# Float32 attention for tiles 3 to 5, and TensorE transposes for the normalized rows of tiles 0 to 2, in a fused attention and gated MLP kernel

## The chip, the cores and the metric

One core of one Trainium2 chip runs the kernel. The metric is the device time of one execution in microseconds. Times inside an execution are counted from the start of its span. Engines are named as in the profile: PE is TensorE, DVE is VectorE, ACT is ScalarE, POOL is GpSimd, SP is SyncE, which issues most transfers.

## The reference

Attention over 4 batches of 8 heads, 768 rows of 64 elements: each row sees its neighbours within 15 rows and 24 block summaries (the elementwise maximum of k over 32 rows, with the mean of v). The result, 3072 tokens of 512 elements, is normalized and goes through a gated MLP.

```python
k_sum = k.reshape(B, H, nb, block, D).max(axis=3)            # block 32, nb 24
v_sum = v.reshape(B, H, nb, block, D).mean(axis=3)
scores_l = np.where(abs(i - j) < 16, scale * q @ k.T, -1e9)  # per batch and head
scores_s = scale * q @ k_sum.T + np.log(block)
a = softmax(concatenate([scores_l, scores_s], axis=-1))
x = (a @ concatenate([v, v_sum], axis=2)).reshape(B * S, H * D)   # heads side by side
xn = x / sqrt(mean(x * x) + 1e-6) * rms_g
g = xn @ w_gate                                              # 512 -> 1536
out = (g * sigmoid(g) * (xn @ w_val)) @ w_out                # 1536 -> 512
```

## The kernel before

The tokens are cut into 24 tiles of 128 rows, six for each batch. A tile passes through scores, softmax and the weighted sum, in two halves of four heads each, then through the normalization (norm_a, norm_b), which leaves its transposed rows in the buffer xT as f16 high and low halves. The MLP takes the tokens in groups of 384, 128, 256 and six times 384; a group has twelve gate_val steps (24 matmuls, 12 for the gate and 12 for the value) and twelve project steps. So the first gate_val needs norm_b of tiles 0, 1 and 2, the first group.

A tile is computed in one of two ways.

- Tiles 0 to 2 (SU = 3) in float32, by the su_ steps. su_k and su_q transpose k and q on PE against an identity. su_scores (matmul L921, masked maximum on DVE at L925, subtraction of the maximum on POOL), su_expo (exponentials on ACT at L934 and L935, then six transposes on PE at L940 and L942, copied out of PSUM by ACT and DVE) and su_attend (matmuls L957 and L960, then three DVE instructions) follow, once for each half. The operands v2f (the rows beside the tile and the v means) are filled by POOL's own transfers (L664), four for each tile, and by su_vsum.
- Tiles 3 to 23 in f16 high and low halves. q, k and v are scaled and split (prep_q, prep_k, prep_v), and k, q and the exponentials are transposed by DMA (kT from khl, qT from qs, eT from ee); the matmuls are L753 in scores and L794 in attend.

The scale of the f16 halves of a batch comes from sums of squares. For batch 0 they are the twelve su_square instructions on ACT (L838), added up on PE at L622; L642 transposes the k maxima back to rows. norm_b of every tile makes high and low halves of the rows (xs, by ACT and by POOL) and transposes them by a DMA on the SP queue (L994).

The gate and value weights sit in the buffer w_gv, in twelve slots of 1024 columns. decode_gv (ACT L457, DVE L458 and L459) and split_gv (PE L493 and L496, ACT L487 and L506, DVE L507) fill one slot each, as the weights come in.

All steps stand in the list PLAN, and tables in ORDER then fix the order of the instructions on each engine; each engine works strictly in that order. ENG says which engine runs a step. The buffers of the first stage are in the pool "start", which is given up before the first gate_val. Among the later buffers the f16 tiles have one for the masked scores (sm) and one for the exponentials (ee), and three PSUM banks named att are shared by all attention steps.

Of the kernel before, what the change touches and what calls it, by code (L numbers as in the profile page):

```python
# [8 lines left out]
F32 = mybir.dt.float32  # L9
# [10 lines left out]
P = 128  # L20
# [9 lines left out]
SU = 3  # L30
SMB = 1
# [3 lines left out]
    sfill="v", susm="p", v2q="p", wgv="a", wo="a", wolo="v", wlo="v", xlo="p", xs="a", w_pow2="p",  # L35
# [16 lines left out]
sum_fold 1 0 0 0; sum_fold 1 0 0 1; prep_k 4; decode_o 2; split_ks 0; decode_gv 5; split_gv 5; prep_q 3; prep_k 5;
fill_k 3; sum_load 1 0 0 2; sum_load 1 0 0 3; sum_load 1 0 1 0; load_gv 7; decode_o 4; decode_gv 6; sum_load 1 0 1 1;
load_o 6; scores 3 0; project 0 0 384 0; sum_fold 1 0 0 2; prep_v 3; gate_val 0 2 384; load_o 8; sum_fold 1 0 0 3;
gate_val 0 3 384; expo 3 0; decode_gv 7; load_gv 8; sum_load 1 0 1 2; load_unit 4; split_gv 6; fill_k 5; decode_o 6;
project 0 1 384 0; scores 3 1; expo 3 1; sum_fold 1 0 1 0; load_gv 9; sum_load 1 0 1 3; sum_fold 1 0 1 1;
sum_fold 1 0 1 2; sum_fold 1 0 1 3; load_o 10; project 0 2 384 0; split_gv 7; sum_load 1 1 0 0; gate_val 0 4 384;
sum_fold 1 1 0 0; sum_load 1 1 0 1; decode_gv 8; project 0 3 384 0; sum_load 1 1 0 2; fill_k 4; sum_scale 1 0;
prep_q 4; split_gv 8; sum_fold 1 1 0 1; sum_load 1 1 0 3; sum_fold 1 1 0 2; project 0 4 384 0; sum_load 1 1 1 0;
load_ks 1; gate_val 0 5 384; gate_val 0 6 384; sum_load 1 1 1 1; attend 3; norm_a 3; sum_fold 1 1 0 3;  # L60
sum_fold 1 1 1 0; project 0 5 384 0; load_unit 5; sum_fold 1 1 1 1; decode_gv 9; scores 4 0; decode_o 8; split_gv 9;
prep_q 5; sum_load 1 1 1 2; load_k 6; expo 4 0; sum_fold 1 1 1 2; split_ks 1; load_gv 10; load_gv 11;
gate_val 0 8 384; decode_gv 10; norm_b 3; gate_val 0 7 384; sum_load 1 1 1 3; scores 4 1; sum_fold 1 1 1 3;
decode_o 10; load_unit 6; swap_att 2; decode_gv 11; gate_val 1 0 128; prep_k 6; project 1 0 128 384; gate_val 1 1 128;
prep_v 4; load_k 7; gate_val 0 9 384; project 0 6 384 0; split_gv 10; project 1 1 128 384; prep_q 6; gate_val 1 2 128;
gate_val 1 3 128; split_gv 11; project 0 7 384 0; scores 5 0; expo 4 1; prep_k 7; fill_k 6; attend 4;
project 1 2 128 384; project 1 3 128 384; norm_a 4; swap_right; scale_h; scores 5 1; load_k 8; sum_load 2 0 0 1;
scores 6 0; scores 6 1; gate_val 1 4 128; load_unit 7; project 0 8 384 0; expo 5 0; sum_scale 1 1; expo 5 1;
project 1 4 128 384; gate_val 1 5 128; project 1 5 128 384; norm_b 4; gate_val 1 6 128; expo 6 0; project 1 6 128 384;
gate_val 1 7 128; expo 6 1; prep_q 7; gate_val 0 11 384; load_k 11; prep_v 5; attend 5; sum_load 2 0 0 0; prep_v 6;  # L70
gate_val 1 8 128; gate_val 0 10 384; project 1 7 128 384; prep_k 8; fill_k 7; norm_a 5; load_unit 8;
project 0 9 384 0; project 0 10 384 0; row_o 0; row_o 1; row_o 2; row_o 3; row_o 4; row_o 5; gate_val 1 9 128;
scores 7 0; gate_val 1 10 128; project 1 8 128 384; norm_b 5; gate_val 1 11 128; load_k 9; prep_q 8; attend 6;
project 1 9 128 384; project 1 10 128 384; scale_o; gate_val 2 0 256; expo 7 0; gate_val 2 1 256; prep_k 9;
swap_att 3; norm_a 6; gate_val 2 2 256; project 1 11 128 384; project 2 0 256 512; project 2 1 256 512; conv_o 0;
scores 7 1; sum_load 2 0 0 2; fill_k 8; project 2 2 256 512; sum_fold 2 0 0 0; sum_fold 2 0 0 1; load_unit 9;
scores 8 0; sum_load 2 0 0 3; load_k 10; prep_v 7; expo 7 1; sum_load 2 0 1 0; sum_load 2 0 1 1; gate_val 2 3 256;
norm_b 6; scores 8 1; gate_val 2 5 256; prep_q 9; project 2 3 256 512; conv_o 1; sum_fold 2 0 0 2; expo 8 0;
sum_fold 2 0 0 3; prep_k 10; prep_k 11; gate_val 2 4 256; expo 8 1; attend 7; sum_load 2 0 1 2; norm_a 7;
gate_val 2 6 256; norm_b 7; prep_v 8; fill_k 10; project 0 11 384 0; sum_fold 2 0 1 0; project 2 4 256 512;  # L80
project 2 5 256 512; conv_o 2; attend 8; fill_k 9; gate_val 2 7 256; sum_fold 2 0 1 1; norm_a 8; project 2 6 256 512;
gate_val 2 8 256; sum_fold 2 0 1 2; norm_b 8; scores 9 0; sum_load 2 0 1 3; gate_val 2 9 256; gate_val 2 10 256;
expo 9 0; sum_load 2 1 0 0; load_unit 10; project 2 7 256 512; conv_o 3; prep_q 10; gate_val 2 11 256; scores 9 1;
sum_fold 2 0 1 3; sum_scale 2 0; gate_val 3 0 384; project 2 8 256 512; sum_load 2 1 0 1; sum_fold 2 1 0 0; load_ks 2;
project 2 9 256 512; conv_o 4; expo 9 1; gate_val 3 1 384; project 2 10 256 512; load_unit 11; split_ks 2;
project 2 11 256 512; conv_o 5; project 3 0 384 768; sum_fold 2 1 0 1; sum_load 2 1 0 2; sum_fold 2 1 0 2;
# [190 lines left out]
def body(tc, q, k, v, wg, wv, wo, rg, out):  # L277
# [19 lines left out]
    with ExitStack() as ctx:  # L297
# [336 lines left out]
        def load_ks(b):  # L634
# [6 lines left out]
            for g in range(NC):  # L641
                nc.tensor.transpose(pt[0:NB, g * P:(g + 1) * P], ks32[:, g, :], ident)  # L642
# [445 lines left out]
```

## Time and profile before

| | |
|---|---|
| time, median of 3 runs | 752.61 us (750.48 to 753.82) |
| profiled execution, own time | 751.9 us |
| its span | 750.1 us |
| mean granted clock of PE | 0.964 |
| PE busy | 685.6 us (91%) |
| DVE busy | 517.5 us (69%) |
| ACT busy | 440.2 us (59%) |
| POOL busy | 260.9 us (35%) |

The own time of the profiled execution holds the span and 1.8 us around it. Busy shares are means over the whole span: what bounds the kernel is seen by stages. The first gate_val starts at 76.12 us; the gate results of the following steps reach DVE (L1014) from 81.14 us on, the ninth at 158.76, the 31st at 254.65, the 43rd at 317.91.

### The profile page before, as it was taken

To read this page: it belongs to the slowest core of one execution; us is meant where nothing else is said; L and a number is where in the kernel's file an instruction comes from. 1 tells how busy PE (TensorE), PEld (TensorE's weight loads), DVE (VectorE), ACT (ScalarE), POOL (GpSimd) and SP (SyncE) were. 2 spreads that over 40 slices of the span, in tenths; PEclk is the share of its full clock that TensorE was granted. 3 is DMA by queue.
4 is the path that set the end of the run, shared out by engine and by line. 5 is a ranking of instruction groups with operands and counts; after the bars stand their busy time and mean duration, and the time that the engine had idled before them with its cause. 6 is when DMAs were issued, how large, how long until landed. Compare 5 with 4: busy or idle time off the path is not lost.

```text
span 750.1 us, 14300 instructions
## 1 busy us (share of the span) xinstructions
PE 685.6 (91%) x4978; PEld 437.7 (58%) x4978; DVE 517.5 (69%) x1507; ACT 440.2 (59%) x936; POOL 260.9 (35%) x347
## 2 busy tenths in 40 slices
PE   3973989388988999999999999999999999999997
PEld 2562556256767786556565556655656555655554
DVE  4598887797678989877678677577757655544223
ACT  2589858776587867756566574657555543522111
POOL 8174113565244564553332253523223312210000
PEclk9995899699999999999999999999999999999999
DMA  9956996559956956687686676765566632221001
GB/s 217 291 197 211 234 254 190 120 108 195 179 94 128 190 119 163 138 174 141 119 168 144 147 155 144 128 138 116 125 113 105 108 78 40 39 50 43 1 0 43
DMA packets 270548, 100.23 MB, mean 134 GB/s; under 512 B 254212, under 2 KB 254308, under 8 KB 270476
## 3 DMA queue, kind: packets, MB, share of 16 engines
q1 hardware_dynamic: 265212, 91.09, 58.0%
q10 hardware_dynamic: 3456, 6.29, 2.3%
q0 software_dynamic: 1808, 1.93, 1.3%
q8 instruction: 39, 0.64, 0.3%
q14 instruction: 33, 0.27, 0.1%
HBM read 51.38 MB, written 6.64 MB: 77 GB/s over the span
## 4 chain that ended last, share of the span: by engine, by line
PE 60%; DMA 9%; DVE 7%; ACT 7%; issue 3%; POOL 2%; SPq 1%; ACTq 0%; POOLq 0%; DVEq 0%
PE gv L1009 37%; PE acc L1038 18%; PE att L753 3%; DMA kT<-khl 2%; DMA eT<-ee 2%; PE att L794 2%; ACT sm L768 1%; DMA qT<-qs 1%; DVE sm L757 1%; DVE hl L357 1%; DMA sum<-hn 1%; POOL ee L357 1%; DMA hn<-in_v_dram 1%; DMA hn<-in_k_dram 1%; ACT ee L352 1%
## 5 line engine op out<-in xcount | busy, mean ns | idle before, releaser
L1009 PE MATMUL gv<-xT,w_gv 128*128 128x384 f16 (+2 forms) x2592 | 407.7, 312 | 13.2 <-DVE th L1014 7.5
L1009 PEld LDWEIGHTS <-w_gv 128*128 128x128 f16 x2592 | 242.5, 99 | 158.9 <-issue 24.1
L1038 PE MATMUL acc<-wo,hh 128*128 128x512 f16 (+1 forms) x576 | 177.0, 389 | 0.0
L357 POOL TENSOR_TENSOR ee<-sm,ee 128x512 f16<-128x512 f32 (+1 forms) x84 | 83.1, 1006 | 134.8 <-ACT ee L352 120.1
L1038 PE MATMUL acc<-wo,hl 128*128 128x512 f16 (+1 forms) x288 | 111.1, 386 | 3.4 <-DVE hl L357 3.4
L1013 ACT ACTIVATE th<-gv,gains 128x384 f32<-128x384 f32 (+2 forms) x108 | 58.2, 539 | 82.2 <-PE gv L1009 78.3
L352 ACT CAST hh<-th 128x384 f16<-128x384 f32 (+3 forms) x108 | 50.8, 470 | 88.0 <-DVE th L1016 44.6
L768 ACT ACTIVATE sm<-sm,mx,c 128x192 f32<-128x192 f32 x168 | 81.6, 537 | 31.2 <-DVE mx L760 22.1
L1014 DVE SCALAR_TENSOR_TENSOR th<-th,gv 128x384 f32<-128x384 f32 (+2 forms) x108 | 54.5, 505 | 64.4 <-ACT th L1013 64.0
L357 DVE TENSOR_TENSOR hl<-th,hh 128x384 f16<-128x384 f32 (+3 forms) x108 | 68.6, 635 | 30.6 <-ACT hh L352 29.8
L1016 DVE SCALAR_TENSOR_TENSOR th<-th,scales,gv 128x384 f32<-128x384 f32 x72 | 44.0, 611 | 36.0 <-PE gv L1009 35.4
L757 DVE CUSTOM_DVE_ANT_0 sm<-att,mask 128x192 f32<-128x192 f32 x168 | 52.6, 350 | 10.7 <-POOL ee L357 5.6
L1038 PEld LDWEIGHTS <-hh 128*128 128x128 f16 x432 | 40.1, 98 | 32.6
L753 PE MATMUL att<-kT,qT 128*128 128x192 f16 x336 | 40.2, 253 | 12.5 <-DMA qT<-qs 9.8
L735 POOL DMA_DIRECT2D v2h<-v2h x42 | 23.0, 547 | 81.6 <-ACT v2h L734 74.6
L357 POOL TENSOR_TENSOR xs<-x,xs 128x512 f16<-128x512 f32 x24 | 31.5, 1314 | 33.8 <-ACT xs L352 33.6
L753 PEld LDWEIGHTS <-qT 128*128 128x128 f16 x336 | 29.3, 100 | 23.4 <-DMA qT<-qs 10.9
L352 ACT CAST ee<-sm 128x512 f16<-128x512 f32 (+1 forms) x84 | 39.6, 506 | 2.6 <-DMA eT<-ee 2.0
L794 PEld LDWEIGHTS <-eT 128*128 128x128 f16 x840 | 34.2, 98 | 11.9 <-issue 1.9
L599 ACT ACTIVATE junk<-hn 96x512 uint8<-96x512 f32 x48 | 30.0, 626 | 16.6 <-DMA hn<-in_v_dram 10.1
L605 POOL TENSOR_TENSOR hn<-hn 96x512 f32<-96x512 f32 x18 | 26.4, 1465 | 31.2 <-DMA hn<-in_v_dram 30.3
L1038 PEld LDWEIGHTS <-hl 128*128 128x128 f16 x216 | 21.1, 98 | 25.5
(190 smaller groups left out, 961.3 us busy)
## 6 DMA issues: line engine op xcount, KB each, us to landing
wo<-in_moe_w_out_dram SPq DMA_DIRECT2D x6, 1024.0 KB
out_dram<-ob ACTq DMA_DIRECT2D x23, 256.0 KB
raw<-in_moe_w_val_dram SPq DMA_DIRECT2D x5, 1024.0 KB
hn<-in_k_dram SPq DMA_DIRECT2D x24, 192.0 KB
hn<-in_v_dram SPq DMA_DIRECT2D x24, 192.0 KB
qr_l<-in_q_dram SPq DMA_DIRECT2D x17, 256.0 KB
vr_l<-in_v_dram SPq DMA_DIRECT2D x17, 256.0 KB
raw<-in_moe_w_gate_dram SPq DMA_DIRECT2D x4, 1024.0 KB
```

The source lines that it names most:

```text
L352: nc.scalar.copy(o, i)
L357: (nc.vector if ENG.get(op, "p") == "v" else nc.gpsimd).tensor_tensor(o, a, b, op=ALU.subtract)
L599: nc.scalar.activation(junk[0:96], y[:, o:o + DM], AF.Square, accum_out=d["ss"][:, j:j + 1])
L753: nc.tensor.matmul(pt[:, j * SC:(j + 1) * SC], lhsT=s["qT"][:, a * H + h, :], rhs=kT[:, h, :], start=(a == 0), stop=(a == 1))
L757: nc.vector.tensor_tensor_reduce(sm[:, i, :], pt[:, j * SC:(j + 1) * SC], mask, 1.0, NEG, op0=ALU.add, op1=ALU.max, accum_out=mx[:, i:i + 1])
L768: nc.scalar.activation(sm[:, i, :], sm[:, i, :], AF.Exp, scale=s["c"][:, 0:1], bias=mx[:, i:i + 1])
L794: nc.tensor.matmul(po[r][:, h // 2, 0:D + 1], lhsT=e, rhs=vv[:, 0:D + 1], start=(n == 0), stop=(n == len(pairs) - 1))
L1009: nc.tensor.matmul(pt[:, 0:T], lhsT=w_gv[:, f - f % 2 + i, wi, c, f % 2, :], rhs=x[:, xi, c, 0:T], start=(n == 0), stop=(n == 3 * NC - 1))
L1013: nc.scalar.activation(th[:, 0:T], pg[:, 0:T], AF.Tanh, scale=f_sc[:, f - f % 2:f - f % 2 + 1])
L1014: nc.vector.scalar_tensor_tensor(th[:, 0:T], th[:, 0:T], 1.0, pg[:, 0:T], op0=ALU.add, op1=ALU.mult)
L1016: nc.vector.scalar_tensor_tensor(th[:, 0:T], th[:, 0:T], sc, pv[:, 0:T], op0=ALU.mult, op1=ALU.mult)
L1038: nc.tensor.matmul(accs[grp][j], lhsT=h[:, js], rhs=wo_hl[f // 2][:, wi, f % 2, :], start=(f == 0 and n == 0), stop=(f == NF - 1 and n == 2))
```

## The change

Tiles 3 to 5, the rest of batch 0, take the float32 path too. Their q, masked scores, exponentials and rows go into buffers of the later stage (kr, vr, qr, sm, ee, eT, x), their PSUM banks are the three att banks, and their k and v operands lie in slots 6 to 11 of w_gv, two slots for each tile, so that decode_gv and split_gv of these slots follow the tile's use. su_scores of these tiles computes heads 0 and 2, then 1 and 3, of a half. What served their f16 path is gone: the su_square steps, the sums of batch 0, load_ks and split_ks of batch 0, prep_k, prep_q, prep_v, scores, expo and attend of tiles 3 to 5. The v means of tiles 3 to 5 are copied by POOL.

norm_b of tiles 0 to 2 (XPE = 3) transposes the float32 rows on PE into PSUM; ACT writes the high half from there and DVE the low half. The copy xs, POOL's subtraction and the DMA transpose fall away for these three tiles. PLAN and the ORDER tables are new. The code moves up by a few lines: L1009 of before is L1008 of after, L921 is L910, L940 and L942 are L929 and L933, L957 and L960 are L947 and L950.

```diff
 SU = 3
+XPE = 3
+SR = 6
+        def su_room(t, name):
+            n = {"k32": 768, "v1f": 528, "v2f": 528}[name]
+            if t < SU:
+                return pools["start"].tile([P, n], F32, name=name, bufs=SU)
+            o = {"k32": 0, "v1f": 768, "v2f": 1296}[name]
+            return w_gv[:, SR + 2 * (t - SU):SR + 2 * (t - SU) + 2]...bitcast(F32)[:, o:o + n]
+        def su_tile(shape, name, other, bufs):
+            if "start" in pools:
+                return pools["start"].tile(shape, F32, name=name, bufs=bufs)
+            return pools["ap"].tile(shape, F32, name=other[0], bufs=other[1])
+        def su_bank(t, name):
+            return ps.tile([P, 512], F32, name=name, bufs={"gv": 2, "acc": 3}[name]) if t < SU else att_tile()
 su_scores
-            sm = pools["start"].tile([P, 4, SC], F32, name="sm", bufs=2)
+            sm = su_tile([P, 4, SC], "sm", ("sm", SMB), 2)
+            for part in ((0, 1, 2, 3),) if t < SU else ((0, 2), (1, 3)):
 norm_b
+            if u < XPE:
+                hi, lo = (xT[grp][:, a, :, off:off + P] for a in range(2))
+                pt = ps.tile([P, 512], F32, name="acc", bufs=3)
+                for c in range(NC):
+                    nc.tensor.transpose(pt[:, c * P:(c + 1) * P], x[:, c * P:(c + 1) * P], ident)
+                pt = pt.rearrange("p (c t) -> p c t", c=NC)
+                copy("xph", hi, pt)
+                sub("xpl", lo, pt, hi)
+                return
```

On POOL, the rows just ahead of the first subtraction of the maximum (sm<-sm,mx). v2f and, in after, part of w_gv are the operands filled by POOL's transfers. Before:

```order
L664 DMA v2f_265<-in_v_dram 24x4x64
L664 DMA v2f_245<-in_v_dram 16x4x64
L898 COPY v2f_245<-ones2_132 64x4x2
L664 DMA v2f_245<-in_v_dram 16x4x64
L664 DMA v2f_245<-in_v_dram 24x4x64
L894 MEMSET v1f_244 128x8x2
L894 MEMSET v1f_264 128x8x2
L664 DMA v2f_245<-in_v_dram 24x4x64
L357 TENSOR_TENSOR sm_251<-sm_251,mx_252 128x768
```

After:

```order
L654 DMA v2f_247<-in_v_dram 24x4x64
L881 MEMSET w_gv_128 128x8x2
L412 CAST v2h_142<-ones2_132 128x4x2
L885 COPY w_gv_128<-ones2_132 64x4x2 x2
L367 AFFINE_SELECT mask0_90<-mask0_90 128x16
L654 DMA v2f_247<-in_v_dram 24x4x64
L654 DMA w_gv_128<-in_v_dram 16x4x64 x2
L654 DMA v2f_162<-in_v_dram 16x4x64
L654 DMA w_gv_128<-in_v_dram 16x4x64 x2
L654 DMA w_gv_128<-in_v_dram 24x4x64
L351 TENSOR_TENSOR sm_257<-sm_257,mx_258 128x768
```

All 24 transfers of six tiles now stand ahead of the first subtraction, where there were the 12 of three tiles; the identity that PE's transposes need (masks.py:199) stands at the 46th place of POOL instead of the 14th.

On PE, the last rows ahead of the first gate_val. Before (kv_ss are the sums of squares, ks the k maxima):

```order
L622 MATMUL att<-kv_ss_152,ones 128x6
L622 MATMUL att<-kv_ss_151,ones 128x6
L642 MATMUL att<-ident,ks_149 24x128 x4
L493 MATMUL att<-w_ss,ones 128x1
```

After (e is the transposed exponentials, x the normalized rows):

```order
L929 MATMUL acc<-ident,se 128x128 x4
L933 MATMUL acc<-ident,se 128x128 x2
L985 MATMUL acc<-ident,x 128x128 x4
L947 MATMUL gv<-v1f,e_651 128x65 x4
L950 MATMUL gv<-v2f,e_651 128x132 x2
L985 MATMUL acc<-ident,x 128x128 x4
L487 MATMUL att<-w_ss,ones 128x1
```

The three steps on the sums and the k maxima are gone; the transposes of the normalized rows stand in their place, the third ones (L985 again) directly ahead of the first gate_val.

On PE in after, behind the fifth half gate step (12 of a step's 24 matmuls) of the first group, where before had nothing but gate_val and project steps; tile 3 is in float32 (qr holds its transposed q, ee its exponentials, w_gv its k):

```order
L929 MATMUL att<-ident,ee 128x128 x4
L933 MATMUL att<-ident,ee 128x128 x2
L910 MATMUL att<-w_gv,qr 128x192 x2
L1037 MATMUL acc<-wo_722,hh 128x512 x2
L1037 MATMUL acc<-wo_722,hl 128x512
L910 MATMUL att<-w_gv,qr 128x192 x2
```

The transposes of the first half's exponentials stand directly ahead of the second half's scores. Between the scores of a half tile and the transposes of its exponentials there stand, for the four half tiles up to the ninth gate_val: two half gate steps and two project steps; three and three; two and three; one and three.

## Rows read from the trace of the kernel before

**Rows 1.** Page, part 2: busy tenths of 40 slices, granted TensorE clock in tenths.
```profile
PE   3973989388988999999999999999999999999997
...
DVE  4598887797678989877678677577757655544223
ACT  2589858776587867756566574657555543522111
...
PEclk9995899699999999999999999999999999999999
```

**Rows 2.** Windows: bounds, length, busy us of each engine, granted clock, DMA share, GB/s.
```profile
0.00:81.10 81.10, 50.74 (x288) 36.24 (x289) 58.81 (x168) 53.55 (x96) 43.88 (x94) 0.84 0.82 226
81.10:158.80 77.70, 59.82 (x378) 38.50 (x377) 63.59 (x151) 55.22 (x105) 25.37 (x31) 0.86 0.76 189
158.80:254.70 95.90, 85.80 (x850) 68.75 (x849) 76.32 (x280) 71.78 (x177) 42.43 (x52) 0.96 0.79 154
254.70:317.90 63.20, 62.67 (x494) 44.36 (x491) 55.62 (x147) 45.67 (x104) 36.59 (x34) 1.00 0.67 140
317.90:750.10 432.20, 426.62 (x2979) 249.89 (x2976) 263.19 (x767) 214.03 (x456) 112.62 (x138) 1.00 0.51 101
```

**Rows 3.** Waits of TensorE from 0 to 81 us: total, times, longest.
```profile
PE att L493 <- ACT w_gv L487: 7.7, 2, 7.5
PE att L622 <- ACT junk L838: 4.9, 1, 4.9
```

**Rows 4.** Windows: TensorE and its clock ahead of the first gate_val.
```profile
60.00:70.00 10.00, 0.97 (x11) 0.71 (x10) 9.06 (x17) 9.52 (x19) 4.17 (x4) 0.50 0.43 127
```

**Rows 5.** Timeline, POOL: start, length, instruction [idle before, releaser].
```profile
18.33 0.60 POOL L664 DMA_DIRECT2D v2f<-in_v_dram  x1 [0.81 <-DMA v2f<-in_v_dram]
22.76 1.47 POOL L357 TENSOR_TENSOR sm<-sm,mx 128x768 f32<-128x768 f32 x1 [3.83 <-DVE mx L925]
...
47.07 1.91 POOL L357 TENSOR_TENSOR sm<-sm,mx 128x768 f32<-128x768 f32 x1 [0.35 <-DVE den L964]
```

**Rows 6.** Groups of POOL instructions: busy us, mean ns | idle before, releasers.
```profile
L664 POOL DMA_DIRECT2D v2f<-in_v_dram x12 | 6.8, 570 | 0.8 <-DMA v2f<-in_v_dram 0.8
```

**Rows 7.** Timeline: first score reduction, first exponential, first weight decoding.
```profile
21.47 0.36 DVE L925 CUSTOM_DVE_ANT_0 sm<-att,mask 128x192 f32<-128x192 f32 x1 [1.51 <-PE att L921]
...
26.39 0.41 ACT L935 ACTIVATE se<-sm 128x256 f32<-128x256 f32 x1
26.52 0.69 DVE L458 TENSOR_SCALAR w<-w 128x1024 uint32<-128x1024 uint32 x1 [0.32 <-ACT w L457]
```

**Rows 8.** Windows: the DVE from the first decoding to the third norm_b.
```profile
26.50:66.40 39.90, 28.87 (x190) 21.15 (x189) 34.54 (x101) 32.44 (x58) 20.47 (x20) 0.85 0.67 217
```

**Rows 9.** Timeline, TensorE: scores, transposes, attend of half tiles in float32.
```profile
42.10 0.93 PE L921 MATMUL att<-k,q 64*128 64x192 f32 x8
42.97 0.66 PE L940 MATMUL acc<-ident,se 128*128 128x128 f32 x4
43.47 0.38 PE L942 MATMUL acc<-ident,se 128*128 128x128 f32 x2
44.78 1.11 PE L957 MATMUL gv<-v1f,e 128*128 128x65 f32 x8 [0.93 <-ACT e L352]
45.72 0.67 PE L960 MATMUL gv<-v2f,e 128*128 128x132 f32 x4
46.23 1.00 PE L957 MATMUL gv<-v1f,e 128*128 128x65 f32 x8
```

**Rows 10.** Timeline: four transposes of float32 rows on TensorE.
```profile
23.72 1.11 PE L885 MATMUL gv<-ident,wo 128*128 128x128 f32 x4
```

**Rows 11.** Timeline, TensorE: the first two gate_val steps.
```profile
76.12 10.83 PE L1009 MATMUL gv<-xT,w_gv 128*128 128x384 f16 x48
```

**Rows 12.** Timeline, TensorE: f16 steps at the full clock.
```profile
164.06 0.62 PE L1038 MATMUL acc<-wo,hh 128*128 128x512 f32 x2
...
164.76 0.62 PE L1038 MATMUL acc<-wo,hh 128*128 128x512 f32 x2
...
168.96 4.07 PE L1009 MATMUL gv<-xT,w_gv 128*128 128x384 f16 x24
172.87 0.82 PE L753 MATMUL att<-kT,qT 128*128 128x192 f16 x8
173.53 0.83 PE L1009 MATMUL gv<-xT,w_gv 128*128 128x128 f16 x12
...
174.96 0.20 PE L794 MATMUL att<-v1h,eT 128*128 128x65 f16 x1
...
175.27 0.71 PE L1038 MATMUL acc<-wo,hh 128*128 128x512 f32 x2
```

**Rows 13.** Timeline, TensorE: the longest wait after the first gate_val.
```profile
143.82 1.46 PE L753 MATMUL att<-kT,qT 128*128 128x192 f16 x8 [9.21 <-DMA qT<-qs]
```

More of the change, by code (lines that the diff above doesn't have):

```diff
@@ L52 @@
[L52 to L86, printed above, removed]
@@ new lines @@
+load_ks 2; project 3 0 384 768; sum_fold 2 1 0 1; project 2 11 256 512; conv_o 5; scores 10 0; prep_v 9;
+gate_val 3 2 384; sum_fold 2 1 0 2; project 3 1 384 768; load_k 14; expo 9 0; sum_load 2 1 0 3; split_ks 2;
+sum_load 2 1 1 0; expo 9 1; sum_load 2 1 1 1; gate_val 3 3 384; sum_fold 2 1 0 3; gate_val 3 4 384; attend 9;
+fill_k 11; norm_a 9; prep_q 11; sum_fold 2 1 1 0; sum_fold 2 1 1 1; scores 10 1; norm_b 9; expo 10 0;
+project 3 2 384 768; gate_val 3 5 384; sum_load 2 1 1 2; gate_val 3 6 384; load_k 12; project 3 3 384 768; prep_v 10;
@@ new lines @@
+gate_val 7 6 384; norm_a 22; norm_b 22; project 7 5 384 2304; scores 23 1; gate_val 7 7 384; expo 23 1;
+project 7 6 384 2304; gate_val 7 8 384; project 7 7 384 2304; gate_val 7 9 384; project 7 8 384 2304; attend 23;
+norm_a 23; gate_val 7 10 384; norm_b 23; project 7 9 384 2304; gate_val 7 11 384; project 7 10 384 2304;
+gate_val 8 0 384; project 7 11 384 2304; gate_val 8 1 384; project 8 0 384 2688; gate_val 8 2 384;
+project 8 1 384 2688; gate_val 8 3 384; project 8 2 384 2688; gate_val 8 4 384; project 8 3 384 2688;
@@ L639, in load_ks @@
                 return
-            pt = att_tile()
-            for g in range(NC):
-                nc.tensor.transpose(pt[0:NB, g * P:(g + 1) * P], ks32[:, g, :], ident)
-            nc.scalar.copy(ksr[0:NB], pt[0:NB, :].rearrange("p (h d) -> p h d", h=H))
         def split_ks(b):
@@ L677, in load_v2 @@
             vp = v[b].rearrange("(g r) s d -> r g s d", r=2)
-            vs = sums[b][1]["sum"].rearrange("(g r n) d -> r n g d", r=2, n=NB)
+            vs = sums[b][1]["sum"].rearrange("(g r n) d -> r n g d", r=2, n=NB) if 1 in parts else None
             before = max(t * P - NP, 0)
@@ L823, in su_first @@
         def su_first():
-            for i in range(2):
-                ss = sp.tile([P, 8], F32, name=f"kv_ss{i}", bufs=1)
-                sums.setdefault(0, {})[i] = dict(ss=ss[:, 0:NTB])
-            sums[0][1]["sum"] = dp.tile([H * NB, D], F32, name="sum1_0")
             band = su["band"] = pools["start"].tile([P, P + NB - 4], F32, name="band")
```

443 lines of the change are left out of this document (226 added, 217 removed).

## The prediction

> **What bounds the kernel now.** I read the page's slices first. From the eleventh slice on PE is at nine tenths or more, and the holes lie in the first fifteen slices, about 280 us [rows 1]. So nothing is decided behind that, and I cut the span by stages with the windows view: up to the first gate result, up to the ninth, the 31st, the 43rd, and the rest [rows 2]. In the last two stages PE is busy for 62.7 of 63.2 us and 426.6 of 432.2 us. Their time is PE's work. The first three are different: PE is idle for 30.4, 17.9 and 10.1 us, and no engine is full. DVE is nearest to full in the first part of the second stage and in the time just ahead of it, ACT as well. There the three engines pass small pieces to each other.
>
> The waits say what the first gate_val waits for. PE waits 7.5 us for w_gv from ACT and 4.9 us for the last square [rows 3], while from 60 to 70 us DVE is busy for 9.1 and ACT for 9.5 of 10 us [rows 4]. ACT is full there partly with the squares which the change removes. After the first gate_val the longest hole is one wait of 9.2 us for a DMA transpose of q [rows 13], which is tile 3's f16 path.
>
> **First stage, to 81.1 us.** The change takes twelve squares from ACT and three matmul steps from PE, and three DMA transposes of rows from SP. It adds three times four transposes on PE at 1.11 us [rows 10] and three high and three low halves on ACT and DVE. But it loads the front of POOL. Before, POOL's last transfer of v2f ends at 18.93 us and it then waits 3.8 us for the first scores [rows 5], so the filling was hidden. After, twelve more transfers stand ahead of the first subtraction; at 0.57 us each [rows 6] they are 6.8 us, and I take 3 us for the fills of tiles 3 to 5 that stand among them. That puts the first subtraction at 18.9 + 6.8 + 3 = 28.7 us instead of 22.8, some 6 us later; a late identity matrix (it now stands behind most of the masks) delays the first scores too, but less than this. The first exponential moves from 26.4 to about 32 us and the first decoding on DVE, which now stands behind the third half tile's reductions, from 26.5 [rows 7] to about 33.7.
>
> From there DVE sets the pace. Between the first decoding and the third norm_b it was busy for 34.5 of 39.9 us, 87% [rows 8]. The order of the changed kernel has nearly the same work in the same place: three low halves and one more decoding step, less seven score reductions that now come earlier, which I sum to 1.6 us more, so 36.1. At the old 87% this lasts 41.6 us and ends at 75.3. The gate_val follows at once: the tail of copy, POOL subtraction, DMA transpose and sums, which took from 66.4 to 76.1 us before, is gone from between. So the first gate_val comes at 75.3 instead of 76.1 us, and the stage gets 0.8 us shorter. What the change wins in the tail is spent at the front. Bounds: with ACT relieved, DVE could run at 95%, as long as nothing else is late, and then the stage is 4.4 us shorter; if the POOL transfers and the late identity cost 5 us beyond my sum, 4 us longer.
>
> One rule of the skill bears on the subtractions on POOL. A subtraction took 1.47 us with DVE in short score reductions, but 1.91 us at 47.07 with DVE at work [rows 5]; for six more half tiles I count at most 0.44 us each, 2.7 us in all, most of it hidden. The Trainium skill, "SBUF — State Buffer", section "Who interferes with whom", says that a DVE instruction with two inputs in SBUF and a GpSimd instruction reading SBUF share a port exclusively, and that the loser waits for the whole instruction. By that rule each of the six could wait out a long DVE instruction of about 1.4 us, by estimate some 8 us. This trace shows the smaller lengthening only.
>
> **Second stage, 77.7 us.** Here the path of tile 3 and most of tile 4 moves from f16 to float32. I count PE's work between the first and the ninth gate result by the order, with start to start times at the full clock: a gate_val step 3.91 us, a project step 0.70, the f16 scores of a half tile 0.66, ten f16 attend matmuls 0.31 and so 0.62 for the twenty of a half tile [rows 12]; the float32 scores of a half 0.87, its transposes 0.88, its attend 1.45, and the transposes of a tile's q 1.11 [rows 9, 10]. Before: 8 x 3.91 + 21 x 0.70 + 4 x 0.66 + 2 x 0.62, with 1.8 us for splitting weights, is 51.7. After: 8 x 3.91 + 18 x 0.70 + 3 x 1.11 + 5 x 0.87 + 4 x (0.88 + 1.45), with 2.2 us for splitting, is 63.1. PE gets 11.4 us more work in a stage in which it idled 17.9. Meanwhile the order takes, by durations of before, some 13 us from DVE's work there and some 14 from ACT's (the f16 splits of k, q and v, the f16 exponentials of four heads one by one), and the wait for q [rows 13] with the DMA transposes.
>
> What is late next is PE itself. To its 63.1 us I add 3.0 for the clock (the first two gate_val steps took 10.83 instead of 7.82, since the clock is at half, 1.2 GHz, after the long idle [rows 4, 11]); four waits of 0.93, in which the attend waits for the copied exponentials as at 44.78 [rows 9], 3.7; and 3 for the waits of gate_val and project on DVE and ACT that remain. That is 72.8 us, a gain of 4.9. Bounds: 66 if no wait remains; and 82, 4 worse than before, where the chain of softmax is not covered (below). The new order of heads, two and two, is not in the trace; it can make the scores 0.4 us dearer per half, a change of stationary operand being all that lies between, or nothing. I take nothing and keep 2 us for the range.
>
> **Third stage, 95.9 us.** Tile 5's float32 halves, five more project steps and fewer f16 halves give PE 4.6 us more work by the same prices, of 10.1 idle; DVE loses 3 us and ACT 7. I take a gain of 1, with 5 to either side. **The fourth** loses some 1 us of PE work that was done earlier, gain 0.7. **The rest** is the same list: 0. DMA gets 17 transposes fewer, among them those of q, k and exponentials of three tiles; I count nothing for the bandwidth.
>
> Sum: 0.8 + 4.9 + 1.0 + 0.7 = 7.4 us. The profiled execution's span of 750.1 becomes 742.7, its own time of 751.9 (the span and 1.8 around it) 744.5. The median of the runs is 0.7 above the profiled execution, so I say 745.
>
> **The rivals.** *The front eats it (same).* POOL's late front and the late identity cost 5 us more than summed, or PE stays at the share it had in the third stage, 85.8 of 95.9 us. Then the second stage's 63.1 + 3.0 last 73.9 and the first stage costs 4: about 750. For it: POOL is at work until 18.9 without a gap, so everything placed there delays. Against: ACT, which was full, has 13 us less to do before the first gate.
>
> *The bare chain (slower).* After the scores of a half tile PE has to wait for four reductions on DVE (from 21.47 to the subtraction at 22.76, 1.3 us), the subtraction on POOL (1.5 to 1.9), and two exponentials (about 0.9 to 1.0 [rows 5, 7]): 4.1 us if no engine is busy. What the order puts on PE between is 2 half gates and 2 projects, 5.3 us; then 8.0, 6.0 and, for the fourth half, 4.1. So the chain is covered as long as each of the three engines takes it up at once. If each is behind one instruction of about 1.4 us, the chain is 8.3 and PE stands for 3.0 + 0.3 + 2.3 + 4.2 = 10 us here and for two more such waits in the third stage, some 7, with the single buffers of masked scores and exponentials holding up the next half, some 5 more: 22 us, about 762 when half a gain elsewhere is left. It decides from a chain of about 7 us on. For it: one buffer each and only three PSUM banks, and PE works in order. Against: DVE and ACT have 13 us less work in just that stage.
>
> *A better front (faster still).* First gate_val at 72 and the second stage at 66: about 734.
>
> *It doesn't do what it says.* The DMA transposes and squares were hidden, since DVE set the first gate_val: the first stage doesn't get shorter. By my sum this is nearly so already, and it alone would give 745 to 746; the gain then comes from the second stage only.
>
> **How the numbers follow.** The forecast with its near variants (740 to 748.8) has 0.42, the better front 0.13, the same about 750 0.27, the bare chain 0.18. A measurement of this kernel can tell 0.5%, 3.8 us, from no change, so from 748.8 to 756.4 counts as the same. Faster 0.55, same 0.27, slower 0.18. The range goes from the better front to the foot of the bare chain: 734 to 759.
>
> **What would show it.** In the changed profile: the first subtraction on POOL at 28 to 30 us; the first gate_val at 72 to 79; PE busy for about 63 to 68 us of a second stage of 70 to 76; no wait of PE above 3 us for the transposes of exponentials (L929) there; no wait for qT until tile 6; the same time from the 43rd gate result to the end, 432. I am wrong if the first gate_val comes after 80 us, or if PE waits on L929 in sum for over 8 us.

## The result and the profile after

The changed kernel takes 734.6 us (median of four runs, 732.4 to 735.7), the kernel before 752.5 us beside it: a ratio of 0.976 (95% interval 0.973 to 0.980). The change makes the kernel 18.0 us faster; the prediction said 745, 7.6 us faster, with a range down to 734. So the direction was right and the size was less than half of what came. The profiled execution took 735.6 us, with a span of 733.8, 16.3 us shorter than the span of before.

In the page, TensorE's row is at nine tenths or more from the fifth slice on, but for two slices and the last, where before it had holes until the thirteenth [rows 1]; its clock is at nine tenths or more from the sixth slice on.

```profile
span 733.8 us, 14113 instructions
PE 693.0 (94%) x4982; PEld 448.1 (61%) x4982; DVE 504.0 (69%) x1465; ACT 413.2 (56%) x873; POOL 248.3 (34%) x358
PE   1986999999898999999999999999999999999997
...
PEclk9975899999999999999999999999999999999999
```

Cut by the same gate results as in [rows 2] (the 1st, the 9th, the 30th and the 42nd; the description of the kernel before and the prediction call the last two the 31st and 43rd, with the right times), the windows view of after reads: bounds, length, busy us of each engine, granted clock, DMA share, GB/s.

```profile
0.00:79.70 79.70, 53.21 (x294) 39.86 (x295) 57.16 (x164) 42.84 (x68) 45.03 (x115) 0.81 0.85 243
79.70:142.00 62.30, 60.18 (x413) 43.03 (x412) 55.20 (x141) 42.98 (x79) 17.41 (x23) 1.00 0.42 129
142.00:238.80 96.80, 90.24 (x801) 70.92 (x801) 73.98 (x241) 67.68 (x164) 41.76 (x48) 0.96 0.65 137
238.80:300.70 61.90, 61.90 (x494) 43.87 (x494) 54.54 (x156) 44.96 (x102) 32.57 (x33) 1.00 0.64 137
300.70:733.80 433.10, 427.49 (x2984) 250.44 (x2981) 263.10 (x769) 214.76 (x462) 111.57 (x141) 1.00 0.51 102
```

| stage | before, us | after, us | difference | predicted |
|---|---|---|---|---|
| first, to the 1st gate result | 81.1 | 79.7 | -1.4 | -0.8 |
| second, to the 9th | 77.7 | 62.3 | -15.4 | -4.9 |
| third, to the 30th | 95.9 | 96.8 | +0.9 | -1.0 |
| fourth, to the 42nd | 63.2 | 61.9 | -1.3 | -0.7 |
| the rest | 432.2 | 433.1 | +0.9 | 0 |

By these cuts nearly all of the gain lies in the second stage. There TensorE has as much to show as before in busy time (60.2 us against 59.8), but it is idle for 2.1 us instead of 17.9, and its granted clock is 1.00 instead of 0.86 [rows 2]. The waits of TensorE in that stage (total, times, longest) are now two, beside 0.9 us of a third that ends at 142.12, just behind the stage:

```profile
PE att L910 <- ACT qr L346: 0.6, 1, 0.6
PE gv L1008 <- DVE th L1013: 0.6, 1, 0.6
```

The same view of before, for its second stage, begins with the wait of [rows 13] and goes on with seven more; the largest are

```profile
PE att L753 <- DMA qT<-qs: 9.2, 1, 9.2
PE gv L1009 <- DVE th L1014: 2.3, 2, 1.3
PE att L753 <- DMA sum<-hn: 2.0, 1, 2.0
PE gv L1009 <- ACT w_gv L506: 1.9, 1, 1.9
```

What such waits cost beyond themselves is seen in the stretches of before's second stage in which the clock was granted at half (0.50, that is 1.2 GHz): the rest of one from the first stage, one behind the wait of 2.0 us, and one that begins within the wait of 9.2 us and lasts to 153.65.

```profile
81.10:81.97 0.87, 0.87 (x4) 0.44 (x3) 0.56 (x1) 0.74 (x4) 0.38 (x1) 0.50 1.04 379
109.28:112.69 3.41, 3.41 (x24) 2.20 (x23) 3.24 (x16) 3.41 (x10) 0.99 (x2) 0.50 0.98 287
136.59:153.65 17.06, 7.03 (x37) 4.25 (x38) 13.40 (x26) 12.52 (x24) 12.80 (x12) 0.50 0.58 128
```

TensorE is busy for 11.3 us in them (0.87, 3.41 and 7.03). At the full clock that work takes about half the time, so by estimate some 5.7 us of the 59.8 busy were lost to the half clock, beside the 17.9 idle. After the change both losses are all but gone from this stage: 15.8 us of idle time and some 5.7 us of clock come back, some 6 us of work come in (60.2 instead of about 54.1), and the balance is the 15.4 us of the table.

One thing qualifies this. The ninth gate result is not the same step in both kernels: in before it belongs to the first group of tokens, in after it is the first of the second group, with 128 columns. The gate matmuls in the second stage (x is their number), before and then after:

```profile
L1009 PE MATMUL gv<-xT,w_gv 128*128 128x384 f16 x201 | 38.0, 347 | 6.3 <-DVE th L1014 2.3 <-ACT w_gv L506 1.9 <-DVE th L1016 1.1
```

```profile
L1008 PE MATMUL gv<-xT,w_gv 128*128 128x384 f16 x168 | 29.5, 326 | 0.6 <-DVE th L1013 0.6
L1008 PE MATMUL gv<-xT,w_gv 128*128 128x128 f16 x12 | 0.8, 219 | 0.0
```

At 3.91 us for 24 [rows 12], the 33 fewer are 5.4 us; with the twelve small ones and one project less, the second stage of after has by estimate some 5 us less of gate and project work, which stands in its first and third stage instead. So some 5 of the 15.4 us are work that moved. The first three stages together hold the same gate steps in both kernels, and there the gain is 15.9 us (238.8 against 254.7): TensorE's idle time falls from 58.3 to 35.2 us, its busy time grows from 196.4 to 203.6 us, more work less the returned clock.

### The profile page after: what moved, and what is told of

It reads as the page before. It is cut to its first block, busy times and chain, and to the rows that moved or that the text cites. A ratio compares the mean times of both kernels' runs of the same rounds, so it can differ in the third digit from the quotient of the medians.

```text
span 733.8 us, 14113 instructions
## 1 busy us (share of the span) xinstructions
PE 693.0 (94%) x4982; PEld 448.1 (61%) x4982; DVE 504.0 (69%) x1465; ACT 413.2 (56%) x873; POOL 248.3 (34%) x358
## 4 chain that ended last, share of the span: by engine, by line
PE 72%; DMA 9%; DVE 8%; ACT 5%; issue 3%; SPq 2%; POOL 1%; ACTq 0%; DVEq 0%; POOLq 0%
PE gv L1008 39%; PE acc L1037 20%; PE att L743 3%; PE att L784 3%; DMA eT<-ee 2%; PE att L910 2%; DMA hn<-in_k_dram 2%; DMA wo<-in_k_dram 1%; DMA hn<-in_v_dram 1%; DVE w L452 1%; ACT sm L758 1%; DVE w L453 1%; DMA qT<-qs 1%; PE gv L843 1%; PE acc L855 1%
## 5 line engine op out<-in xcount | busy, mean ns | idle before, releaser
L1008 PE MATMUL gv<-xT,w_gv 128*128 128x384 f16 (+2 forms) x2592 | 405.1, 311 | 3.9 <-DVE th L1013 1.1
L1008 PEld LDWEIGHTS <-w_gv 128*128 128x128 f16 x2592 | 240.8, 99 | 148.3 <-issue 16.1
L351 POOL TENSOR_TENSOR ee<-sm,ee 128x256 f16<-128x256 f32 (+1 forms) x72 | 68.2, 963 | 108.3 <-ACT ee L346 93.0
L351 DVE TENSOR_TENSOR hl<-th,hh 128x384 f16<-128x384 f32 (+3 forms) x108 | 70.1, 651 | 35.2 <-ACT hh L346 34.9
L758 ACT ACTIVATE sm<-sm,mx,c 128x192 f32<-128x192 f32 x144 | 69.3, 536 | 35.8 <-DVE mx L750 32.4
L747 DVE CUSTOM_DVE_ANT_0 sm<-att,mask 128x192 f32<-128x192 f32 x144 | 45.6, 350 | 25.9 <-PE att L743 19.2
L725 POOL DMA_DIRECT2D v2h<-v2h x36 | 19.5, 543 | 81.3 <-ACT v2h L724 80.2
L346 ACT CAST ee<-sm 128x512 f16<-128x512 f32 (+1 forms) x72 | 34.2, 506 | 4.2 <-DMA eT<-ee 3.7
L743 PE MATMUL att<-kT,qT 128*128 128x192 f16 x288 | 33.7, 249 | 2.5 <-DMA qT<-qs 2.5
L784 PEld LDWEIGHTS <-eT 128*128 128x128 f16 x720 | 29.0, 97 | 10.9 <-DMA eT<-ee 2.1
L351 POOL TENSOR_TENSOR xs<-x,xs 128x512 f16<-128x512 f32 x21 | 25.1, 1197 | 24.9 <-ACT xs L346 24.8
L743 PEld LDWEIGHTS <-qT 128*128 128x128 f16 x288 | 24.8, 99 | 11.5 <-DMA qT<-qs 3.0
```

The costliest lines, as they stand in the source:

```text
L346: nc.scalar.copy(o, i)
L351: (nc.vector if ENG.get(op, "p") == "v" else nc.gpsimd).tensor_tensor(o, a, b, op=ALU.subtract)
L743: nc.tensor.matmul(pt[:, j * SC:(j + 1) * SC], lhsT=s["qT"][:, a * H + h, :], rhs=kT[:, h, :], start=(a == 0), stop=(a == 1))
L747: nc.vector.tensor_tensor_reduce(sm[:, i, :], pt[:, j * SC:(j + 1) * SC], mask, 1.0, NEG, op0=ALU.add, op1=ALU.max, accum_out=mx[:, i:i + 1])
L758: nc.scalar.activation(sm[:, i, :], sm[:, i, :], AF.Exp, scale=s["c"][:, 0:1], bias=mx[:, i:i + 1])
L784: nc.tensor.matmul(po[r][:, h // 2, 0:D + 1], lhsT=e, rhs=vv[:, 0:D + 1], start=(n == 0), stop=(n == len(pairs) - 1))
```

## Experiments

All were timed in three rounds against the kernel before. Three theories were put to them for the second stage: that the removed DMA round trips (q and exponentials through a transfer) give the gain, called the latency theory; that the time freed on DVE and ACT gives it; and, on the risk, whether the chain from scores to exponentials is covered with room or just in time. Others ask what the TensorE transposes in norm_b are worth, and what sets the front.

### Work put back on DVE and on ACT

`dve_back` adds 19 idle reductions to DVE in the second stage, `act_back` 17 idle squares to ACT; about as much as the change took from each.

```diff
+        def pad_v(n):
+            nc.vector.tensor_reduce(pad["v"], gb, axis=AX.X, op=ALU.max)
+        def pad_a(n):
+            nc.scalar.activation(junk, gb, AF.Square, accum_out=pad["a"])
```

> The changed kernel with 19 idle reductions of 128x512 on DVE (about 0.69 us each, 13.1 us in all) spread between the first and the ninth gate result: the DVE time that the float32 path took out of that stage is put back, and no transfer. They read the gain row and their result is used by nobody. Engine time theory (the second stage fell by 15.3 us because DVE and ACT had 13 and 14 us less to do): the time rises by 10 to 13, to 745 to 748. Latency theory (it fell because the float32 path has no DMA transpose between the splitting of k, q or the exponentials and their use): only what DVE can't hold, 55.2 + 13.1 = 68.3 of 62.3 us, so plus 4 to 8, 738 to 743.

> The changed kernel with 17 idle squares of 128x512 on ACT (0.81 us each with the reading of the sum, 13.8 us in all) spread over the same stage. Engine time theory: plus 5 to 10, 740 to 745. Latency theory: ACT is then busy 43.0 + 13.8 = 56.8 of 62.3 us, so plus 0 to 3, 734 to 738.

Measured: `dve_back` 744.2 us (0.989, 0.985 to 0.993), 9.6 us more than the change; `act_back` 734.8 us (0.976, 0.972 to 0.981), no difference. The second stage of each, by windows, `dve_back` first:

```profile
82.10:152.60 70.50, 62.62 (x420) 44.07 (x419) 65.02 (x159) 43.73 (x80) 15.34 (x21) 0.98 0.36 112
```

```profile
79.50:143.60 64.10, 60.41 (x412) 42.99 (x412) 55.12 (x141) 53.47 (x113) 17.26 (x23) 1.00 0.40 125
```

With 10.5 us more on ACT the stage is 1.8 us longer and the total the same: ACT's relief is not where the gain comes from. With 9.8 us more on DVE (65.0 against 55.2, close to before's 63.6) it is 8.2 us longer. The total, 9.6 us more, is between what the two theories said. DVE's freed time is a condition of about half of the gain, then: at 65.0 of 70.5 us DVE is the fullest engine of the stage, ahead of TensorE with 62.6.

### The round trips put back

`trip_q` sends the transposed q of tiles 3 to 5 out to DRAM and back before it is used, `trip_e` the transposed exponentials of their six half tiles. Of the two calls in the diff each kernel has one, for tiles 3 to 5 alone. It stands for what a DMA transpose would hold up, not for the same transfer.

```diff
+        def trip(x, n):
+            d = dp.tile([P, n], F32, name="trip", bufs=2)
+            nc.sync.dma_start(d, x.rearrange("p a b -> p (a b)"))
+            nc.sync.dma_start(x.rearrange("p a b -> p (a b)"), d)
...
+                trip(qT, DM)
...
+                trip(eT, 6 * P)
```

> The changed kernel in which the transposed q of tiles 3, 4 and 5 goes out to device memory and back by two transfers on the SP queue before the scores read it: no engine gets more work, a transfer's delay comes into the path, as the DMA transpose of q had been. Latency theory: each tile's scores come 2 to 4 us late, since PE has 2 to 3 us of work between the transposes of q and the scores and a trip lasts 5 or more, so plus 5 to 12, 740 to 747. Engine time theory: plus 0 to 2, 734 to 737.

> The changed kernel in which the transposed exponentials of the six half tiles of tiles 3 to 5 go out and back in the same way. The first half's have 9 to 12 us until the attend, the second half's 1 to 4. Latency theory: three waits of 2 to 5 us, plus 7 to 13, 741 to 748. Engine time theory: plus 0 to 2, 734 to 737.

Measured: `trip_q` 757.8 us (1.007, 1.003 to 1.011), `trip_e` 770.6 us (1.025, 1.020 to 1.030): 23 and 36 us more than the change. The direction is the latency theory's, the size is about two and three times the upper end of what it said (12 and 13 us). `trip_q`'s waits and window show why:

```profile
PE att L911 <- DMA qr<-trip: 18.7, 3, 7.7
```

```profile
79.50:166.40 86.90, 67.58 (x409) 46.67 (x409) 52.73 (x141) 43.46 (x80) 17.11 (x23) 0.86 0.35 110
```

Three waits of up to 7.7 us are 18.7, and the same work takes 67.6 us of TensorE instead of 60.2, at a granted clock of 0.86. Those are the two kinds of loss that before had: of the 67.6 us, 17.5 lie in stretches of half clock. One wait in `trip_q`'s timeline, TensorE (start, length, instruction, and in brackets the idle time before):

```profile
90.30 1.66 PE L911 MATMUL att<-w_gv,qr 64*128 64x192 f32 x8 [7.73 <-DMA qr<-trip]
91.89 4.02 PE L1014 MATMUL gv<-xT,w_gv 128*128 128x384 f16 x12
...
97.48 2.12 PE L1014 MATMUL gv<-xT,w_gv 128*128 128x384 f16 x12
```

Behind the wait twelve gate matmuls take 4.02 us, a little later the same twelve 2.12. The Trainium skill ("TensorE: Matmul & The Clock Gate", section "HAM oscillation — how this bites in real kernels") tells of a kernel in which each wait for a transfer throws the engine back to the low clock and every wait pays this again; these rows agree. In `trip_e` the waits for eT come to 20.9 us, 13.6 of them in the second stage, where another 5.0 us go to one wait for exponentials and the clock is 0.85.

### The chain of softmax made longer

The prediction's slower rival said that the chain from the scores of a half tile to its exponentials is covered by two half gates and two projects, and decides from about 7 us on. `chain_1` puts one idle copy on POOL behind each subtraction of tiles 3 to 5 (0.8 to 1.2 us), `chain_3` three (2.9 to 4.7 us; its diff is shown).

```diff
+            for _ in range(3 if t >= SU else 0):
+                nc.gpsimd.tensor_copy(sm, sm)
```

> The changed kernel with one more POOL instruction (a copy of the masked scores onto themselves, 128x768, 1.2 to 1.5 us) behind each subtraction of the maximum of the six half tiles of tiles 3 to 5. Cover theory (the prediction's count: a chain of 4.1 us, and 5.3, 8.0, 6.0 and 4.1 us of work on PE over it): 0 to 2 us more, 734 to 737. Just in time theory (the changed kernel's trace: the exponentials end 0.2, 1.0, 0.1, 0.7, 0.8 and 0.0 us before PE takes them up, since DVE and ACT have other work between): each half tile comes 0.3 to 1.4 us late, plus 4 to 7, 738 to 742.

> The same with three such copies, some 4 us more in each half tile's chain. Cover theory: plus 7 to 11, 742 to 746. Just in time theory: each half tile 3 to 4 us late, 20 us of waiting on PE and the half clock behind some of it, less what the other engines catch up: plus 15 to 24, 750 to 759.

Measured: `chain_1` 735.0 us (0.977, 0.974 to 0.980), no difference; `chain_3` 757.7 us (1.008, 1.005 to 1.011), 23 us more. So a chain longer by about 1 us costs nothing that can be measured, as the cover theory said, and where it is longer by some 4 us the whole gain is gone, as the just in time theory said; where between the two it turns was not tried. In its profile `chain_1` does wait: its second stage is 2.3 us longer than the change's (64.6, as much as its waits below), and its third is 2.6 us shorter (94.2). The waits of `chain_1` and of `chain_3` for the exponentials (second and third stage in the latter), and the second stage of `chain_3`:

```profile
PE att L930 <- ACT ee L924: 2.3, 4, 1.0
```

```profile
PE att L930 <- ACT ee L924: 18.0, 5, 4.0
```

```profile
80.50:160.50 80.00, 68.17 (x419) 47.69 (x418) 58.25 (x140) 42.86 (x80) 31.23 (x33) 0.89 0.32 98
```

In the changed kernel itself the first such chain reads, POOL, ACT and TensorE (timeline views):

```profile
86.02 1.47 POOL L351 TENSOR_TENSOR sm<-sm,mx 128x768 f32<-128x768 f32 x1 [0.20 <-DVE mx L914]
```

```profile
87.69 0.62 ACT L923 ACTIVATE ee<-sm 128x512 f32<-128x512 f32 x1
88.22 0.40 ACT L924 ACTIVATE ee<-sm 128x256 f32<-128x256 f32 x1
```

```profile
82.66 0.93 PE L910 MATMUL att<-w_gv,qr 64*128 64x192 f32 x8
...
86.87 2.12 PE L1008 MATMUL gv<-xT,w_gv 128*128 128x384 f16 x12
88.83 0.60 PE L929 MATMUL att<-ident,ee 128*128 128x128 f32 x4
89.27 0.38 PE L933 MATMUL att<-ident,ee 128*128 128x128 f32 x2
```

The scores end at 83.6, the exponentials at 88.6, and TensorE takes them at 88.8: a chain of 5.0 us under 5.2 us of gates and projects. The six chains of the three tiles end 0 to 1.0 us before they are needed.

### The transposes of the normalized rows, alone and taken away

`xpe_alone` is the kernel before with the new branch in norm_b and nothing else. `no_xpe` and `no_xpe_2` are the changed kernel with the DMA transposes back; in `no_xpe` they stand on the SP queue ahead of the loads of the output weights, in `no_xpe_2` behind them. The diff is that of the latter two; besides it only ORDER changes.

```diff
-XPE = 3
+XPE = 0
```

> The kernel before with nothing but the transposes of the normalized rows of tiles 0 to 2 on TensorE. The first gate_val of before waits for squares, the k maxima and the weights of slot 5, which stay: minus 1 to plus 1, 751 to 754. If the DMA transposes held it by themselves: minus 3 to 6, 746 to 750.

> The changed kernel with the normalized rows of tiles 0 to 2 transposed by DMA as before (high half by ACT, low half by POOL, transfer on the SP queue), all else as it is. If the transposes by TensorE set the first gate_val (the trace: PE waits for the normalized rows, and takes them up at once): the last tile needs POOL's 1.5 us, and a transfer of some 4 us, instead of 2.4 us on PE, ACT and DVE, and SP's loads stand behind it: plus 3 to 6, 738 to 741. If it was hidden, as the prediction has it: 0 to 1, 734 to 736.

> As no_xpe, but with the three DMA transposes behind the three loads of the output weights on the SP queue, which in the changed kernel issue until 68.1 us because they wait for DVE to free their buffers. In no_xpe the first transpose stood ahead of them, waited for its rows until 61.8 and moved the loads 9.6 us back, and with them the decoding on which ACT and the weights of a slot depend. If that was its cost: the gate_val comes when the third transpose lands, about 75 to 78 instead of 72 us, plus 3 to 6, 738 to 741. If the transposes by DMA themselves are dear: plus 10 or more, 745 up.

Measured: `xpe_alone` 754.2 us (1.002, 1.000 to 1.004); `no_xpe` 751.6 us (0.999, 0.996 to 1.002); `no_xpe_2` 747.4 us (0.992, 0.989 to 0.994). `no_xpe` missed both of its expectations, in part since the queue position held up the loads as well; `no_xpe_2` has that mended and is still 12.8 us slower than the change, the dearer of its two cases. The first gate_val of `no_xpe_2` on TensorE, and its SP queue:

```profile
83.30 6.76 PE L1007 MATMUL gv<-xT,w_gv 128*128 128x384 f16 x24 [14.43 <-DMA xT<-xs]
```

```profile
67.36 13.93 SPq L992 DMA_TRANSPOSE xT<-xs  x3
```

Three DMA transposes through one buffer xs follow each other over 13.9 us, and the first gate_val waits 14.4 for them. Its second stage (91.2 to 154.0) lasts 62.8 us, as in the change and with the same order of steps: the shorter second stage belongs to the float32 path. What the TensorE transposes do is keep the first stage at 79.7 instead of 91.2 us. In the order of before they bring nothing (`xpe_alone`), in the new order 12.8 us. An order made for the DMA transposes might lose less; it was not tried.

### The front

Two kernels move what stands at the late start, the POOL transfers and the identity that the prediction named, and the loads that it did not: `loads_first` builds the identity first on POOL and loads k and q ahead of the large weights, `v2_late` moves the twelve POOL transfers of tiles 3 to 5 behind the six subtractions. `front_both` does both. Only the ORDER tables change.

> The changed kernel with the same work, but the identity matrix made first on POOL, and on the SP queue the k and q rows that PE needs first ahead of a v tile and of a 1 MB load of weights. Trace reading (PE starts at 14.16 us because the k rows of tile 1 were issued sixth, at 4.7 us, and landed at 14.0; POOL's transfers run until 26.85 us, and the first subtraction starts at 27.25): PE starts at 9 to 10 us, but POOL is not ready earlier, so 0 to minus 2, 732 to 735. If the loads set the front: minus 3 to 6, 728 to 732.

> The changed kernel with POOL's twelve transfers for tiles 3 to 5 moved behind the six subtractions of tiles 0 to 2. By the prediction's step (the front of POOL delays the first subtraction by 6 us and DVE's work by as much): minus 4 to 6, 728 to 731. By the trace (the scores of the first half tile come at 26.8 us anyway, POOL waits 0.4 us for them): 0 to minus 1, 733 to 735.

> Both together: the loads in the new order, the identity first, the twelve transfers late. If the front is a chain of loads, PE, DVE and POOL that has to be shortened at both places: first subtraction at 21 to 23 us instead of 27.25, the first gate_val 3 to 5 us earlier, 729 to 732, faster than both kernels. If DVE waits for the weights' loads (now later by some 3 us) instead: 733 to 736.

Measured: 735.0 us (0.977, 0.973 to 0.981), 734.9 us (0.977, 0.973 to 0.981), and 731.1 us (0.971, 0.967 to 0.975) for both together. The first subtraction on POOL, in this order:

```profile
28.66 2.90 POOL L350 TENSOR_TENSOR sm<-sm,mx 128x768 f32<-128x768 f32 x2
```

```profile
27.34 1.47 POOL L350 TENSOR_TENSOR sm<-sm,mx 128x768 f32<-128x768 f32 x1 [7.14 <-DVE mx L913]
```

```profile
24.48 1.47 POOL L350 TENSOR_TENSOR sm<-sm,mx 128x768 f32<-128x768 f32 x1 [4.21 <-DVE mx L913]
```

With early loads POOL comes from its transfers without a pause; with late transfers POOL stands idle for 7.1 us until the scores come. The first gate result of these two comes later than the change's, at 81.24 and 83.25 us, though their total is the same. Either holds the front alone, and only both together move it: the first gate result comes at 75.95 instead of 79.70 us, and the time is 3.8 to 3.9 us less than that of the two others, on the same chip. This is the fastest kernel of the case, though its interval still overlaps with those of the change and of the two others.

## Why the prediction was right in direction and short in size

- **What bounds the kernel.** Right: nothing behind the first three stages changed by more than 1.4 us, and what the change moved lies in the stages before, where the engines pass small pieces to each other. The slices were misread by a little: the twelfth and thirteenth of before are at eight tenths [rows 1], so the nine tenths begin with the fourteenth, not the eleventh.
- **First stage, 0.8 us shorter.** It got 1.4 us shorter, within the bounds, but partly by luck. The first gate_val comes at 72.04 (said 75.3, before 76.12). From there to the first gate result it takes 7.7 us and not before's 5.0: ACT takes up the gate at 78.75 and DVE at 79.70, behind their decoding work. The two misses, 3.3 us early and 2.7 us late, nearly cancel. The stations ahead of it were near: first subtraction at 27.25 (said 28.7), first decoding on DVE at 31.61 (33.7). But the reason was half right. The POOL transfers were taken as the main cause of the late front, with the identity behind them; `v2_late` and `loads_first` show that the start of TensorE holds it as long. TensorE's first transposes wait until 14.16 us for the loads of k; the identity, which `loads_first` moves as well, was ready at 12.29.

```profile
PE gv L843 <- DMA wo<-in_k_dram: 14.2, 1, 14.2
```

- **Second stage, 72.8 us.** This is the step that failed: it came to 62.3, 10.5 us less. The sum had four terms, and all of them were too large.
  - *The waits*, 6.7 in all, are the largest miss: *four waits of 0.93 us* on copied exponentials, 3.7, and *3 us of other waits* came to 2.1 idle together. The new order copies the second half's exponentials while the first half's attend runs, so the wait of [rows 9] doesn't arise (rows below).
  - *The clock*, 3.0, was 0 in this stage. The clock is at half until 78.04, and the stage begins with the first gate result at 79.70. The term was misplaced to begin with: in before too, all but 0.87 us of that half clock lay ahead of the first gate result (81.10 to 81.97).
  - *The work*, 63.1, was 60.2. The transposes of a tile's q were priced at 1.11 us by [rows 10] and took 0.60 here, 1.5 us for three tiles; the price was one of the half clock (last section). The sum also took eight gate_val steps (192 matmuls) and 18 projects, where the trace has 168 matmuls of 384 columns, twelve of 128 and 20 projects, by the prediction's prices some 1.7 us less.

```profile
100.13 0.60 PE L929 MATMUL att<-ident,ee 128*128 128x128 f32 x4
100.56 0.38 PE L933 MATMUL att<-ident,ee 128*128 128x128 f32 x2
100.78 1.00 PE L947 MATMUL att<-w_gv,eT 128*128 128x65 f32 x8
101.62 0.67 PE L950 MATMUL att<-w_gv,eT 128*128 128x132 f32 x4
102.13 1.00 PE L947 MATMUL att<-w_gv,eT 128*128 128x65 f32 x8
```

  The bound of 66 "if no wait remains" was still too long, by the 3.0 us for the clock and the 2.9 us of work. A sign of the clock stood in the prediction's own numbers: it counted 51.7 us of work in before's stage, which showed 59.8 busy [rows 2], and did not ask for the 8.1 between. Some 5.7 of them are the half clock by the estimate above, and 1.3 are the eight or nine gate matmuls above its count of 192; the rest is open.
- **Third stage, 1.0 us shorter.** It got 0.9 longer, within the 5 us given. TensorE's busy time grew by 4.4 us (said 4.6) and the idle time fell from 10.1 to 6.6, but the agreement is chance: by the counts some 3 us of the growth are the gate matmuls that the ninth result leaves to this stage. In seven of the eleven kernels built from the change the stage took 92 to 94 us, so part of the 0.9 belongs to this one execution.
- **Fourth stage and rest.** 1.3 shorter and 0.9 longer, against 0.7 shorter and 0.
- **The front eats it.** Fell: the first stage was not longer.
- **The bare chain.** It did not happen, but it was a real risk: `chain_1` costs nothing, `chain_3` 23 us, where the prediction said 22 us for a chain of 8.3. That the sizes are so close is partly luck, since the rival had no half clock in its sum and `chain_3` has (0.89 in its second stage, with chains of 7.8 to 10.0 us). The shipped chain is 5.0 us, 0.9 more than the 4.1 said.
- **A better front.** It gave 734, the measured time, for first gate_val at 72 and 66 us of second stage. The first came true (72.04), but only 1.4 of its 4.1 us reached the first gate result; the second stage was shorter still, and the stages behind it gained less than said. So the right total is made of errors that cancel.
- **It doesn't do what it says.** Its premise holds in before's order (`xpe_alone`: nothing gained), but not in the new one, where the transposes on TensorE are worth 12.8 us. The prediction's argument that they were nearly hidden was made on before's order and carried to another.

**What carries the gain.** The float32 path shortens the second stage by 15 us (some 5 of them moved work), with or without the TensorE transposes. That needs two things at once: no wait of a transfer's length on TensorE (`trip_q`, `trip_e`) and DVE's freed 8 us, worth 9.6 us of the total (`dve_back`). It does not need ACT's freed time. The TensorE transposes then keep the first stage from getting 11 us longer. Four kernels show how the two parts go together: before 752.5, the transposes alone 754.2, the float32 path alone 747.4 in the better of two orders, both 734.6. What stays open: no kernel here takes the DMA steps out of the kernel before, so whether an f16 path in another order could lose its waits is not known; the round trips of the experiments were put in, which shows what such a wait costs, not that each one of before cost the same.

## What to carry to other kernels

A wait on TensorE is priced with what follows it: read the granted clock behind it, since here about a quarter of the loss stood in the busy time and not in the idle time (in `trip_q` 7.4 us beside 18.7 us of waits). A chain that is just covered may have a microsecond of room, and beyond it the loss comes at every step, with the clock on top. Where two orders are cut at the same number of results, see that the same steps lie between the cuts. And a part that gains nothing alone may be what lets the other part count, so test both alone and together.

## What the runs showed of the hardware

- A 256 KB round trip of q through DRAM takes 9.0, 6.2 and 5.9 us in `trip_q`. In the first, the transfer out is issued at 81.31, the one back, which waits for it, at 87.43, and TensorE goes on at 90.30.

```profile
81.31 0.35 SPq L960 DMA_DIRECT2D trip<-qr  x1
87.43 0.34 SPq L961 DMA_DIRECT2D qr<-trip  x1
```

- The prediction held the lengthening of POOL's subtractions to 0.44 us, by [rows 5], against a rule of the Trainium skill ("SBUF — State Buffer", section "Who interferes with whom") that the loser of the shared port waits for the whole instruction. The changed kernel's rows agree with the rule. In the second stage a subtraction starts at 95.59 beside a DVE subtraction of two operands that began at 95.34:

```profile
95.59 2.30 POOL L351 TENSOR_TENSOR sm<-sm,mx 128x768 f32<-128x768 f32 x1 [8.10 <-DVE mx L914]
```

```profile
95.34 1.22 DVE L351 TENSOR_TENSOR wo<-w,wo 128x1024 fp32r<-128x1024 f32 x1
```

  The next DVE instruction starts at 96.47, 0.88 us after POOL's start, and POOL's takes 0.83 us more than the 1.47 of the one at 86.02. In the other direction, DVE's L452, which takes 0.69 us at 97.91, takes 1.66 at 86.38, while the subtraction of 86.02 runs to 87.49. All of this stays hidden here: none of the six chains is late by it.
- Four transposes of float32 rows take 1.08 us at the start of the changed program, 1.09 at 68.49 and 0.60 at 79.12. At 68.49 the granted clock is 0.50, at 79.12 it is 1.00.

```profile
14.16 1.08 PE L843 MATMUL gv<-ident,wo 128*128 128x128 f32 x4 [14.16 <-DMA wo<-in_k_dram]
...
68.49 1.09 PE L985 MATMUL acc<-ident,x 128*128 128x128 f32 x4 [5.73 <-DVE x L978]
...
79.12 0.60 PE L873 MATMUL att<-ident,vr 128*128 128x128 f32 x4
```

  The windows view reads 1.00 at the start as well, but the trace's list of granted clocks begins only at 23.43 us (in before at 30.77), and a time without an entry is shown as 1.00. By its durations the start ran at the half clock. The kernel before agrees: eight score matmuls (L921) take 1.65 us at 19.78 and 0.93 at 42.10 [rows 9]. So the 1.11 us of [rows 10], taken at 23.72, is a price of the half clock, which the prediction used for the full one.
